# Attention scores and values by turns in the first unit of an attention and feed-forward kernel

## The chip, the cores and the metric

The kernel runs on one core of one Trainium2 chip. The metric is the device time of one execution in microseconds; the kernel before takes 1377.58 us (median of three runs, 1377.35 to 1379.76). A profiled execution spans 1376.2 us.

Names of engines: PE is the matrix engine (PEld its weight loads), ACT the scalar engine, DVE the vector engine, POOL GpSimd, SP the engine that issues DMA transfers. PE writes only to PSUM, which the kernel uses as eight banks of 128 partitions by 512 fp32 numbers, `banks[0]` to `banks[7]`.

## The reference

Attention with normalized q and k over 8 batches of 12 heads, 448 positions, 64 features, and behind it a feed-forward block with a squared ReLU. All is fp32.

```python
q_n, k_n = rmsnorm(q, g_q), rmsnorm(k, g_k)     # (8, 12, 448, 64)
scores = scale * np.matmul(q_n, k_n.transpose(0, 1, 3, 2))
attn = np.exp(scores - max); attn = attn / (sum(attn) + 1e-09)
x = np.matmul(attn, v)  # -> (8 * 448, 12 * 64) = (3584, 768)
h = np.maximum(x @ w_in, 0.0)                   # w_in (768, 2048)
out = h * h @ w_out                             # w_out (2048, 768)
```

## The kernel before, in words

**Pairs.** The unit of attention work is a pair of heads of one batch: 48 pairs, `i` = 0 to 47, six for each batch. The 128 partitions hold the two heads' 64 features (for q and k turned to features by positions), or 128 positions. A pair's 448 keys are three blocks of 128 (`m` = 0, 1, 2) and 64 last ones; the last keys of an even pair and of the odd pair behind it share one tile (`m` = NJ = 3). For a block, `score(i, m)` multiplies k and q into two banks (one for each head e), keys on the partitions; `weigh(i, m)` lets ACT read both banks and write the exps to two `wT` tiles (L466; a ring of eight). There is no maximum to subtract as long as the gains are small (`shift` is False; that is the path that runs). `attend(i, (n,))` multiplies the weights of a block with v and adds up in the values' bank (bank 4). `additions(i)` lets POOL add the weights of the blocks up (L485, two `sum` tiles), `denominators(i)` multiplies these sums with ones (L620), so that each sum stands in all 64 partitions of its head, and DVE transposes the bank by blocks (`take_sums`, L662). `invert(i)` takes reciprocals of one number for each position and spreads them again, and `finish(i)` multiplies the values with them.

**Order.** The order of all instructions is written out by hand. A feed-forward unit works on two batches; while its matmuls run, the attention of the next two batches is laid between them. `run(until)` takes steps of the feed-forward stream (a Python generator whose steps have costs) until a due place, and small tasks (queues `tasks`, `pool_tasks`) with each step. The stream of the first unit (L1021 matmuls for the first product, L1200 and L1286 for the second) also converts the weights: they arrive as 64-bit words by DMA (L1424, L1429) and three ACT steps (L1443, L1444, L1446) and two DVE steps (L1457, L1476) make fp32 of each piece.

Pairs 0 to 12 come ahead of the first unit. The attention of pairs 13 to 24 lies in the first unit (130 to 483 us of the span), in two half visits for each pair (`visit_among(i, n)`, n = 0 and 1), at equal distances of cost. Pairs 25 to 47 (`whole(i)` is `i > 24`) lie in the second unit in one visit each, `visit_whole(i)`.

**A first half visit** (n = 0) of pair i: values of blocks 0 and 1 of pair i-1, then scores and exps of blocks 0 and 1 of pair i. **A second half visit** (n = 1): values of block 2 of pair i-1, for odd i also the last keys of both pairs i-1 and i (`attend_both`, L586, which writes the odd pair's part to bank 2 and lets ACT copy it to a tile `rest`, L593), then score and exps of block 2 and, for even i, of the last keys, for which q and k of pair i+1 must be there. Some half a visit's distance ahead of the second half visit, between feed-forward products, stand `denominators(i - 1)`, in bank 3. Also just ahead of a second half visit stands the turning of the next pair's q (DVE, L370) and its scaling by ACT (L380).

**Shapes on PE.** In these visits a score of a block is two matmuls of 64 rows (features of a head) by 128 columns (keys), one for each head (L458); values are two of 128 rows (keys) by 64 columns (L550). Scores of block m go to banks 0 and 1 (m even) or 2 and 3 (m odd).

**The second unit before** already works in quarters: there a score is four matmuls of 64x64 (two heads, two halves of the keys, L447), values are four too (`attend_halves`, L565): the two halves of the keys add up in two banks, 4 and 3 (`second_bank`), which `join_halves` (L574 to 578) adds: for odd pairs DVE adds `rest` and then the second bank; for even pairs ACT copies `rest` from bank 0 and the values from bank 4 (L576, L577), then DVE adds the second bank (L578). `finish` then multiplies on POOL (L708), where the other form does it on DVE (L713, L715). In a visit, values of block m of pair i-1 and the score of block m of pair i take turns; the scores of blocks 0, 1, 2 and the last keys go to banks (0, 1), (2, 0), (1, 2) and (0, 4).

`joint(i)` (L280) says that a pair's values are in two banks; it is `whole(i - i % 2 + 1)`, so true from pair 24 on. `sums_bank(i)` (L525) is bank 3 in the first unit.

Of the kernel before, what the change touches and what calls it, by code (L numbers as in the profile page):

```python
# [26 lines left out]
NJ = 3  # L27
# [198 lines left out]
def program(ctx, tc, rows, v, g, wide, ones, moe_w_in, moe_w_out, out, shift):  # L226
# [50 lines left out]
    def whole(i):  # L277
        return i > 2 * 2 * NPAIR

    def joint(i):  # L280

        return whole(i - i % 2 + 1) and not shift

    def slots_of(i, n):

# [14 lines left out]
    def alone(i):  # L300

        return pairs[i][0] < 2
# [131 lines left out]

    def banks_of(i, m):

        if whole(i) and not shift:
            return [banks[n][:, 0:S] for n in ((0, 1), (2, 0), (1, 2), (0, 4))[m]]
        return [banks[m % 2 * 2 + e][:, 0:S] for e in range(2)]

    def score(i, m):

        scs = banks_of(i, m)
        if whole(i) and m < NJ:
            for e, sc in enumerate(scs):
                for half in range(2):
                    nc.tensor.matmul(  # L447
                        sc[ds(half * D, D)],
                        lhsT=turned[i, 1][ds(e * D, D), ds(m * P + half * D, D)],
                        rhs=turned[i, 0][ds(e * D, D), :], start=True, stop=True,  # L450
                    )
            return
        for p in (i, i + 1) if m == NJ else (i,):
            some = ds(p % 2 * LASTS, LASTS) if m == NJ else ds(0, P)
            keys = ds(m * P, LASTS if m == NJ else P)
            for e, sc in enumerate(scs):
                r = ds(e * D, D)
                nc.tensor.matmul(  # L458
                    sc[some], lhsT=turned[p, 1][r, keys], rhs=turned[p, 0][r, :],
                    start=True, stop=True,  # L460
                )
# [60 lines left out]
                nc.vector.tensor_copy(out=tiles[NJ][e][mine, part], in_=tr[mine, NJ, :size])  # L522

    def sums_bank(i):
        return banks[4 + (i + 1) % 2 if alone(i) else 2 if whole(i + 1) else 3][:, 0:S]  # L525

    def values_bank(i):
# [89 lines left out]
    def denominators(i):  # L617

        for e in range(2):
            nc.tensor.matmul(  # L620
                sums_bank(i)[ds(e * D, D), :], lhsT=ones, rhs=sums.pop((i, e)),
                start=True, stop=True,
            )
        take_sums(i)
# [1142 lines left out]

    def visit_among(i, n):
        run_all()
        if not shift:  # L1770
            if n and i - 1 not in inverse:
                denominators(i - 1)
            attend(i - 1, (2 * n, 2 * n + 1))
            forget(i - 1, (2 * n, 2 * n + 1))
        elif n == 0:
            attend_all(i - 1)
        if n == 0 and i <= last:
            load_v(i)
        if i <= last:
            weigh_slots(i, n)  # L1780
        if n and not shift:
            tasks.append(lambda: invert(i - 1))
            tasks.append(lambda: finish(i - 1))
        if n and i <= last and not shift:
            additions(i)
        if n == 0:
            prepare(i + 2)
            run_tasks(2)
            tasks.appendleft(lambda: None)
        elif whole(i + 1):  # L1790
            prepare(i + 3)

    def room_for_squares(i):

# [75 lines left out]
    with tc.manual_schedule(engines=ENGINES):  # L1870
# [8 lines left out]
        for i in range(len(pairs) + 1):  # L1879
            for n in range(1 if whole(i) else VISITS):  # L1880
                at = i * VISITS + n - VISITS - unit
                if at < 0:
                    visit_alone(i, n)
                    continue
                u, x = divmod(at, unit)
                if x == 0:
                    u, x = u - 1, unit
                run(place(u, x - (1 if whole(i - 1) else 0.5)))
                if i < last:
                    if whole(i) and not shift:  # L1890
                        tasks.append(partial(lambda i: turn_blocks(i + 1, 1), i))
                        tasks.append(partial(lambda i: turn_blocks(i + 1, 0), i))
                        tasks.append(partial(lambda i: load_qk(i + 4), i))
                    else:
                        for some in (1, 0) if whole(i) else (1 - n,):
                            turn_among(i + 1, some)
                        if n or whole(i):
                            tasks.append(lambda i=i: load_qk(i + 4))
                    if n and first and x > 1 and not shift:
                        denominators(i - 1)  # L1900
                run(place(u, x))
                if x == unit:
                    closing = whole(i)
                    drain()
                    stream, spent, first = ffn(u + 1), 0, u < 0
                    if shift:
                        run(COST if first else LATER)
                    elif first:
                        run(COST_IN + 1)
                slowly = x < unit  # L1910
                if whole(i):
                    visit_whole(i)
                else:
                    visit_among(i, n)
# [35 lines left out]
```

## Time and profile before

| what | value |
|---|---|
| median of three runs | 1377.58 us |
| span of the profiled execution | 1376.2 us |
| granted PE clock over the span | 0.999 |
| PE busy | 1351.8 us, 98% |
| ACT, DVE, POOL busy | 45%, 60%, 58% |
| first unit's stretch with attention (125 to 483 us): PE busy | 353.59 of 358 us |
| matmul lines of the visits there | L458 and L550, L586, L620 |
| the same in the second unit | L447, L565, L586, L458, L629 |

A busy PE here means that matmuls follow each other; shares are averages over stages, so the visits are looked at one by one: start of the first attention matmul to start of the first feed-forward matmul behind it. In a row of the timeline stand start, length, engine, line, operation, out<-in, shape, and in brackets idle time of the engine just before it and what ended that; several instructions of a kind are merged (x8). An fp32 matmul shows as two MATMUL instructions.

### The profile page before, as it was taken

What the parts mean: (1) busy time and instruction counts of PE and PEld (TensorE: products, weight loads), DVE (VectorE), ACT (ScalarE), POOL (GpSimd) and SP (SyncE); (2) the same over time, 40 slices, a digit from 0 to 9 for tenths busy, and PEclk for the clock granted to TensorE, in tenths of its full rate; (3) what the DMA queues carried; (4) which work ended last, traced back from release to release, by engine and by line L of the source; (5) the groups of instructions that cost most, each with busy time, mean ns of one, the idle gap of its engine ahead of it and who ended that gap; (6) DMA issues with size and microseconds to landing.
All of it is one profiled execution on the core that took longest, in us unless ns stands there. A gap on an engine that the chain in (4) does not pass through costs nothing.

```text
span 1376.2 us, 19610 instructions
## 1 busy us (share of the span) xinstructions
PE 1351.8 (98%) x6320; PEld 844.0 (61%) x6320; DVE 819.2 (60%) x1647; ACT 614.6 (45%) x1130; POOL 792.1 (58%) x792
## 2 busy tenths in 40 slices
PE   7999999999999999999999999999999999999998
PEld 3333444444444476677768586766767777868684
DVE  4897555877767765455547755455556642544454
ACT  6995476757757244442434244443524032203030
POOL 5668664755656878576767887565846630303030
PEclk9999999999999999999999999999999999999999
DMA  5665846977859866674748575665527441515133
GB/s 137 172 180 152 206 110 166 255 194 204 253 135 280 253 173 207 155 206 107 222 99 242 166 201 163 150 198 144 175 70 240 149 166 65 172 57 184 40 126 105
DMA packets 394372, 229.82 MB, mean 167 GB/s; under 512 B 271892, under 2 KB 355988, under 8 KB 393236
## 3 DMA queue, kind: packets, MB, share of 16 engines
q1 hardware_dynamic: 393968, 228.41, 58.8%
q8 instruction: 52, 0.85, 0.3%
q14 instruction: 60, 0.49, 0.1%
q10 hardware_dynamic: 292, 0.07, 0.0%
HBM read 171.05 MB, written 57.34 MB: 166 GB/s over the span
## 4 chain that ended last, share of the span: by engine, by line
PE 86%; DVE 3%; POOL 3%; issue 2%; ACT 2%; DMA 2%; SPq 1%; POOLq 0%; ACTq 0%; DVEq 0%
PE bank L1286 31%; PE bank L1077 25%; PE bank L1021 8%; PE bank L565 4%; PE bank L447 4%; PE bank L458 4%; PE bank L550 3%; PE bank L1200 2%; PE bank L586 1%; DMA in_sb<-in_deep 1%; PE bank L629 1%; PE bank L602 1%; PE bank L620 1%; DVE acc L1383 1%; SPq L159 1%
## 5 line engine op out<-in xcount | busy, mean ns | idle before, releaser
L1077 PE MATMUL bank<-xT,in_sb 128*128 128x224 f32 x1344 | 288.0, 353 | 0.0
L1286 PE MATMUL bank<-out_sb,hid 128*128 128x384 f32 x768 | 273.0, 488 | 2.0 <-POOL out_sb L1552 1.4
L1383 DVE TENSOR_TENSOR acc<-acc,bank 128x384 f32<-128x384 f32 x312 | 166.3, 548 | 160.0 <-PE bank L1286 131.4
L1077 PEld LDWEIGHTS bank<-xT,in_sb 128*128 128x128 f32 x1344 | 252.9, 190 | 10.4 <-ACT wT L466 5.6
L466 ACT ACTIVATE wT<-bank,rr 128x448 f32<-128x448 f32 x288 | 164.0, 632 | 157.9 <-PE bank L447 97.9
L1286 PEld LDWEIGHTS bank<-out_sb,hid 128*128 128x128 f32 x768 | 144.6, 190 | 104.4 <-issue 6.3
L1286 PE MATMUL bank<-out_sb,sums 128*128 128x384 f32 x576 | 207.0, 490 | 1.1 <-DVE acc L1383 0.7
L204 POOL TENSOR_TENSOR rr<-ms,minus_half 128x8 f32<-128x8 f32 (+1 forms) x96 | 145.3, 1514 | 69.1 <-DVE ms L197 65.8
L1062 DVE TENSOR_TENSOR hid<-hid,bank 128x224 f32<-128x224 f32 x312 | 111.3, 384 | 83.0 <-PE bank L1077 77.9
L1286 PEld LDWEIGHTS bank<-out_sb,sums 128*128 128x128 f32 x576 | 107.7, 190 | 86.0 <-DVE acc L1383 4.1
L1021 PE MATMUL bank<-xT,in_sb 128*128 128x448 f32 x336 | 131.7, 545 | 0.0
L485 POOL TENSOR_TENSOR sum<-sum,wT 128x448 f32<-128x448 f32 (+1 forms) x96 | 112.5, 1194 | 7.6 <-ACT wT L466 6.1
L458 PE MATMUL bank<-qT,kT 64*128 64x448 f32 (+1 forms) x492 | 102.4, 571 | 3.5 <-ACT qT L380 2.4
L1021 PEld LDWEIGHTS bank<-xT,in_sb 128*128 128x128 f32 x336 | 62.1, 190 | 68.8 <-issue 60.9
L1130 POOL TENSOR_TENSOR hid<-hid 128x448 f32<-128x448 f32 x24 | 27.3, 1144 | 123.1 <-DVE hid L1062 118.7
L485 POOL TENSOR_TENSOR sum<-wT 128x448 f32<-128x448 f32 x48 | 55.9, 1185 | 68.6 <-ACT wT L466 68.6
L1134 ACT ACTIVATE hid<-hid 128x448 f32<-128x448 f32 x96 | 55.0, 573 | 72.3 <-DVE hid L1062 48.4
L447 PE MATMUL bank<-qT,kT 64*64 64x448 f32 x552 | 75.1, 540 | 0.0
L1077 PE MATMUL bank<-more,in_sb 128*128 128x224 f32 x288 | 74.3, 353 | 0.0
L458 PEld LDWEIGHTS bank<-qT,kT 64*128 64x128 f32 (+1 forms) x492 | 35.3, 166 | 63.4 <-issue 37.1
L1074 ACT COPY hid<-bank 128x448 f32<-128x448 f32 x24 | 12.8, 533 | 136.9 <-PE bank L1077 136.1
L565 PE MATMUL bank<-wT,vt 64*64 64x448 f32 x576 | 73.3, 544 | 0.0
(142 smaller groups left out, 2063.1 us busy)
## 6 DMA issues: line engine op xcount, KB each, us to landing
out_sb<-out_forms SPq DMA_DIRECT2D x80, 384.0 KB, 5.2
in_sb<-in_deep SPq DMA_DIRECT2D x64, 384.0 KB, 4.1
in_sb<-in_deep SPq DMA_DIRECT2D x80, 256.0 KB, 4.2
words<-in_moe_w_in_dram SPq DMA_DIRECT2D x32, 384.0 KB, 3.9
words<-in_moe_w_out_dram SPq DMA_DIRECT2D x32, 384.0 KB, 3.6
out_forms<-out_sb SPq DMA_DIRECT2D x8, 1536.0 KB, 6.6
qk<-in_q_dram SPq DMA_DIRECT2D x96, 96.0 KB, 2.8
qk<-in_k_dram SPq DMA_DIRECT2D x96, 96.0 KB, 2.8
```

Of the source, the lines that this page charges most:

```text
L204: self.nc.gpsimd.tensor_tensor(out=self.rr[i][:, x, 0 : self.count(i)], in0=ms, in1=self.minus_half.to_broadcast(list(ms.shape)), op=ALU.pow,)
L447: nc.tensor.matmul(sc[ds(half * D, D)], lhsT=turned[i, 1][ds(e * D, D), ds(m * P + half * D, D)], rhs=turned[i, 0][ds(e * D, D), :], start ...
L458: nc.tensor.matmul(sc[some], lhsT=turned[p, 1][r, keys], rhs=turned[p, 0][r, :], start=True, stop=True,)
L466: nc.scalar.activation(new_weights((i, m), e), sc, AF.Exp, scale=rows.rr[i][:, 1, 2 * m + e : 2 * m + e + 1],)
L485: nc.gpsimd.tensor_tensor(out=sums[i, e][some], in0=left[some], in1=weights[key_of(i, m), e][some], op=ALU.add)
L565: nc.tensor.matmul(bank[ds(e * D, D), :], lhsT=values[i][keys, n, e, :], rhs=weights[(i, n), e][keys], start=n == 0, stop=n == NJ - 1 and ...
L1021: nc.tensor.matmul(ps, lhsT=w_sb[:, IN.index(left), c, :], rhs=forms[u, c][right], start=first and c == 0, stop=c == NK - 1, skip_group_ch ...
L1062: nc.vector.tensor_tensor(out=quarter(name, n), in0=quarter(base, n), in1=ps, op=ALU.add)
L1077: nc.tensor.matmul(ps, lhsT=left, rhs=right, start=start, stop=stop, skip_group_check=True)
L1134: nc.scalar.activation(dst, dst, AF.Relu)
L1286: nc.tensor.matmul(ps, lhsT=extra[left][:, t] if tt == NT else lefts[left][:, t, ts(tt, P)], rhs=w_sb[t][:, OUT.index(right), :], start=fi ...
L1383: nc.vector.tensor_tensor(out=acc, in0=acc, in1=ps, op=ALU.add)
```

## The change

Pairs 13 to 24 get the form of the second unit, in their two half visits:

- `quartered(i)`, `i > 12`, takes the place of `whole(i)` in `joint`, `banks_of` and `score`, so scores are quarters in banks (0, 1), (2, 0), (1, 2), (0, 4), and values from pair 12 on are halves in banks 4 and 3, with `join_halves` and POOL's multiplication in `finish`.
- A new `visit_quarters(i, n)` issues a half visit. n = 0: values 0, score 0, values 1, score 1, each score followed by its exps. n = 1: values 2, score 2, then for odd i both pairs' last values, then `join_halves(i - 1)`, for even i the score of the last keys, and at the end `denominators(i - 1)`.
- These denominators go to bank 1 in place of bank 3, and no longer stand ahead of the second half visit between feed-forward products.
- `load_v(i)` is called behind the first half visit's matmuls; nothing else is moved.

```diff
+    def quartered(i):
+        return i > 2 * NPAIR
+
     def joint(i):
-        return whole(i - i % 2 + 1) and not shift
+        return quartered(i - i % 2 + 1) and not shift
...
     def banks_of(i, m):
-        if whole(i) and not shift:
+        if quartered(i) and not shift:
             return [banks[n][:, 0:S] for n in ((0, 1), (2, 0), (1, 2), (0, 4))[m]]
...
     def score(i, m):
         scs = banks_of(i, m)
-        if whole(i) and m < NJ:
+        if quartered(i) and m < NJ:
...
     def sums_bank(i):
+        if joint(i) and not whole(i + 1):
+            return banks[1][:, 0:S]
         return banks[4 + (i + 1) % 2 if alone(i) else 2 if whole(i + 1) else 3][:, 0:S]
...
     def visit_among(i, n):
         run_all()
-        if not shift:
+        if quartered(i) and not shift:
+            visit_quarters(i, n)
+        elif not shift:
...
-        if i <= last:
+        if i <= last and (shift or not quartered(i)):
             weigh_slots(i, n)
...
+    def visit_quarters(i, n):
+
+        for m in range(NJ)[2 * n : 2 * n + 2]:
+            attend(i - 1, (m,))
+            forget(i - 1, (m,))
+            score(i, m)
+            weigh(i, m)
+        if n == 0:
+            return
+        if i % 2:
+            attend(i - 1, (NJ,))
+            forget(i - 1, (NJ,))
+        join_halves(i - 1)
+        if i % 2 == 0:
+            score(i, NJ)
+            weigh(i, NJ)
+        denominators(i - 1)
...
-                    if n and first and x > 1 and not shift:
-                        denominators(i - 1)
```

## The prediction

> **What bounds the kernel now.** The page comes first, for what the time hangs on.
>
> ```profile
> span 1376.2 us, 19610 instructions
> PE 1351.8 (98%) x6320; PEld 844.0 (61%) x6320; DVE 819.2 (60%) x1647; ACT 614.6 (45%) x1130; POOL 792.1 (58%) x792
> PE 86%; DVE 3%; POOL 3%; issue 2%; ACT 2%; DMA 2%; SPq 1%; POOLq 0%; ACTq 0%; DVEq 0%
> ```
>
> PE is busy for 98% of the span and carries 86% of the chain that ended last: a microsecond in which it stands still or works longer is a microsecond of the kernel. So I asked next, by windows, how long each attention visit of the first unit holds PE, from its first matmul to the first feed-forward matmul behind it. The first half visits of pairs 13 to 24 (pair 13's, those of pairs 17, 20 and 23, the sum of all twelve; a row is window, length, then busy PE, PEld, DVE, ACT, POOL):
>
> ```profile
> 131.54:134.90 3.36, 3.36 (x17) 1.17 (x16) 0.75 (x2) 0.54 (x1) 3.16 (x3) 1.00 0.59 94
> ...
> 246.74:250.10 3.36, 3.36 (x18) 1.18 (x17) 3.36 (x5) 1.31 (x3) 3.36 (x3) 1.00 0.96 231
> ...
> 335.14:338.50 3.36, 3.36 (x18) 1.17 (x17) 3.36 (x5) 0.03 (x1) 3.36 (x4) 1.00 1.05 271
> ...
> 424.98:428.34 3.36, 3.36 (x17) 1.17 (x16) 3.36 (x5) 2.69 (x5) 3.36 (x3) 1.00 1.13 305
> ...
> sum 40.32, PE 40.32 PEld 14.10 DVE 22.71 ACT 10.54 POOL 25.11; mean PE 3.36 PEld 1.17 DVE 1.89 ACT 0.88 POOL 2.09
> ```
>
> The sum is twelve times 3.36, with PE busy throughout and whatever the other engines do: here PE waits for nobody. Values of two key blocks come first, then two scores, which go to banks 0 to 3 that ACT emptied long ago. The second half visits, odd pairs, then even pairs:
>
> ```profile
> 141.86:145.94 4.08, 4.08 (x21) 1.30 (x20) 2.74 (x5) 1.20 (x2) 4.00 (x5) 1.00 0.96 284
> ...
> 260.41:263.18 2.77, 2.77 (x18) 0.71 (x17) 2.59 (x6) 2.27 (x5) 0.00 (x0) 1.00 1.15 433
> 320.90:323.67 2.77, 2.77 (x18) 0.71 (x17) 2.59 (x4) 1.22 (x3) 2.34 (x2) 1.00 1.05 297
> ...
> 438.66:441.43 2.77, 2.77 (x18) 0.71 (x17) 2.59 (x6) 1.87 (x4) 0.00 (x0) 1.00 1.05 346
> sum 17.93, PE 17.93 PEld 4.85 DVE 14.04 ACT 9.93 POOL 11.81; mean PE 2.99 PEld 0.81 DVE 2.34 ACT 1.66 POOL 1.97
> ```
>
> ```profile
> 171.18:175.79 4.61, 3.72 (x18) 0.89 (x17) 4.37 (x9) 3.71 (x7) 1.36 (x2) 1.00 0.11 25
> 231.78:235.26 3.48, 3.48 (x17) 0.89 (x16) 3.26 (x8) 2.06 (x4) 0.46 (x2) 1.00 1.03 286
> 291.53:294.30 2.77, 2.77 (x17) 0.71 (x17) 2.77 (x5) 1.48 (x3) 2.77 (x4) 1.00 0.78 191
> ...
> 470.01:472.78 2.77, 2.77 (x18) 0.71 (x17) 1.89 (x5) 1.49 (x3) 2.69 (x3) 1.00 0.46 94
> sum 22.33, PE 19.95 PEld 4.98 DVE 20.74 ACT 15.89 POOL 9.88; mean PE 3.33 PEld 0.83 DVE 3.46 ACT 2.65 POOL 1.65
> ```
>
> The odd ones are 2.77 us (pair 13's 4.08 holds its denominators too). The even ones run from 2.77 (pairs 18 and 24) to over 4.61; what lengthens them is priced below.
>
> **The new form where nothing is late.** The second unit of the same run already works by turns on quarters, so its timeline prices the new form: one visit, with the exps of its first score.
>
> ```profile
> 483.29 0.98 PE L565 MATMUL bank<-wT,vt 64*64 64x448 f32 x8
> 484.09 0.93 PE L447 MATMUL bank<-qT,kT 64*64 64x448 f32 x8
> 484.85 0.93 PE L565 MATMUL bank<-wT,vt 64*64 64x448 f32 x8
> 485.14 1.16 ACT L466 ACTIVATE wT<-bank,rr 128x448 f32<-128x448 f32 x2 [4.04 <-PE bank L447]
> 485.83 0.97 PE L447 MATMUL bank<-qT,kT 64*64 64x448 f32 x6
> ```
>
> A group (the values or the score of one key block) takes 0.80 us at the start of a visit and 0.76 each behind another. The second score writes banks 2 and 0, and bank 0 still holds the first score's first head. The exp that empties it starts 1.85 us into the visit (485.14), and the second score's second head starts 0.69 after that, at 2.54 (485.83), though its turn was at 0.80+2x0.76 = 2.32. So even here, where ACT had nothing else to do (4.04 us of idle time ahead of the exp), PE is held a little by ACT. Three more rows give what follows a late start, and what denominators cost by themselves:
>
> ```profile
> 174.89 0.97 PE L458 MATMUL bank<-qT,kT 64*64 64x448 f32 x4 [0.89 <-ACT qT L380]
> ...
> 463.41 0.97 PE L620 MATMUL bank<-sum,ones 128*64 128x448 f32 x4
> 464.31 1.88 PE L1286 MATMUL bank<-out_sb,sums 128*128 128x384 f32 x5
> ```
>
> Quarters that start afresh at 174.89 hold PE until 175.79, the end of that window: 0.90. Denominators, both heads in two passes, hold it 0.90 too (463.41 to 464.31).
>
> **First half visits.** Four groups by turns replace four groups in a row: the same number of passes through the array, with twice the instructions for a score. With ACT free the visit is 2.54+0.90 = 3.44 long in place of 3.36: +0.08. So the turns gain nothing here, and they put an exp into PE's path. PE takes its instructions in order (in pair 14's window, 171.18, it runs 3.72 of 4.61 us and none of the feed-forward matmuls fills the rest): when the second score's second head waits, so do all matmuls behind it, and through them DVE and ACT. What counts now is when the first exp can run:
>
> ```profile
> ACT wT L466 <- PE bank L458: 28.9, 11, 13.7
> 135.52 0.64 ACT L466 ACTIVATE wT<-bank,rr 128x448 f32<-128x448 f32 x1 [3.34 <-POOL sum L485]
> 248.76 0.56 ACT L1443 ACTIVATE words<-words 128x384 f32<-128x384 f32 x1 [2.89 <-DMA words<-in_moe_w_out_dram]
> 250.64 1.67 ACT L466 ACTIVATE wT<-bank,rr 128x448 f32<-128x448 f32 x3
> ...
> 338.47 0.56 ACT L1443 ACTIVATE words<-words 128x384 f32<-128x384 f32 x1 [4.19 <-DMA words<-in_moe_w_out_dram]
> 340.33 2.20 ACT L466 ACTIVATE wT<-bank,rr 128x448 f32<-128x448 f32 x4
> ...
> 426.60 1.07 ACT L1446 ACTIVATE words<-words 128x384 f16<-128x384 f32 x1
> ```
>
> In the first unit ACT's exps mostly waited for their scores (11 waits), ACT having nothing else to do; so I count eight visits at 0.08, 0.64. Four are late. Pair 13: POOL still reads the weights that the exp overwrites, exp at 135.52, 3.98 into the visit; with 0.69 until bank 0 is written and 0.90 from there it makes 5.57, +2.21. Pairs 17 and 20: three ACT steps on a weight load that is still landing stand ahead of the exp, which starts at 3.90 and 5.19: 5.49 and 6.78, +2.13 and +3.42. Pair 23: those steps end at 427.67, 2.69 in: 4.28, +0.92. In the trace of before these late exps cost nothing: no matmul of the visit needs them. First half: 0.64+2.21+2.13+3.42+0.92 = +9.3 us.
>
> **Second half visits, odd pairs.** Three groups (values, score, both pairs' last values), and then the denominators that stood by themselves ahead of the visit. They go to bank 1, which holds the third score's first head, so they too wait for an exp. Promptly: exp at 1.85, denominators from 2.54 to 3.44; before, 2.77+0.90 = 3.67. But ACT scales the next pair's q ahead of that exp:
>
> ```profile
> 263.41 0.65 ACT L380 ACTIVATE qT<-qT,g 128x448 f32<-128x448 f32 x1
> 322.84 0.67 ACT L380 ACTIVATE qT<-qT,g 128x448 f32<-128x448 f32 x1 [1.55 <-DVE qT L370]
> 441.66 0.65 ACT L380 ACTIVATE qT<-qT,g 128x448 f32<-128x448 f32 x1
> ```
>
> It ends 3.65 into the visits of pairs 17 and 23 and 2.61 into pair 19's. With 0.69+0.90 behind it: 5.24, 5.24 and 4.20. The other three I take as prompt, 3x3.44 = 10.32; were they as late as pair 19's, it would be 2.3 more. After 25.0, before 17.93+5x0.90 = 22.43: +2.6 us.
>
> **Second half visits, even pairs.** The last score needs the next pair's scaled q:
>
> ```profile
> 233.64 0.67 ACT L380 ACTIVATE qT<-qT,g 128x448 f32<-128x448 f32 x1 [1.42 <-DVE qT L370]
> ```
>
> In pair 16's visit q is ready at 234.31, and the visit ends 0.95 later, at 235.26; in pair 14's PE waits 0.89 for it outright (174.89). q's time is set by DVE and ACT, which the change leaves as they are up to there, so four visits end when they did, and the denominators behind them find bank 1 read. Only pairs 18 and 24 (2.77) can be shorter: three groups are 0.80+0.76+0.90 = 2.46, but the last score's second head goes to the values' bank, and DVE must have read that. Between 0 and 0.3 each; I take 0.1: -0.2 us.
>
> **Work that moves.** POOL gets a multiplication for each pair in place of DVE's. The denominators, now behind the visit instead of ahead of it, keep the two sum buffers longer, which POOL's next additions need. POOL's queue stops at both.
>
> ```profile
> L708 POOL TENSOR_TENSOR xT<-xT,inverse x12: 1127/1137/1525, 519.2 to 1076.5; 128x448 f32<-128x448 f32 x12
> POOL sums L1186 <- ACT hid L1170: 42.7, 8, 8.4
> ```
>
> That is 12x1.14 = 13.7 us more on an engine that stood 42.7 us waiting for ACT in this stretch. I take 0, that wait being the cover; without it see the last rival. For even pairs ACT copies one more bank (not longer than a late exp's 0.64) beside feed-forward matmuls: 0. DVE stands at the transposition of the sums until the denominators are done, and the feed-forward additions stand behind it; the feed-forward part has three banks in turn, so I take 0. The loads of v are issued behind the visit's instructions now, but nothing else is issued on SP's queue in between: 0. Bounds of all this together: -2 (PE's delays let loads land in time for the next exp) and +5.
>
> **Sum.** 9.3+2.6-0.2 = +11.7 us on the span of 1376.2, so 1387.9; the median, 1377.58, lies 1.4 above that span, so 1389.3.
>
> **Rivals.** *Faster: the change of shape is what costs.* The groups at 484.09 and 484.85 are 0.76 apart without a change of shape; four such are 3.04, so the three changes of shape in a 3.36 visit cost 0.32, or 0.1 each. If ACT were never waited for, first halves would be 2.32+0.90 = 3.22 (12x0.14 = 1.7 saved), odd second halves 2.46+0.90 = 3.36 (22.43-6x3.36 = 2.3), even ones 0.6 less: 4.6 saved, 1373.0. It decides if the exp is over by 2.3 us into a visit; 485.83 says that it isn't even in the quiet second unit. 6%. [...]
>
> *No difference: the four late exps go away*, as PE's own delays give POOL and the loads time. Then 12x0.08 = +1.0, odd pairs 6x3.44-22.43 = -1.8, even -0.2: -1.0, 1376.6. Against it: ACT's three steps follow feed-forward work that shifts with PE. 10%.
>
> *Slower still: POOL's queue.* In pairs 14, 17, 20 and 23 second products follow the visit and read sums from POOL:
>
> ```profile
> 183.63 2.74 PE L1286 MATMUL bank<-out_sb,sums 128*128 128x384 f32 x8
> ```
>
> That is 12.4 us after 171.18. If the four sums stand behind the multiplication and two additions, POOL starts it at some 5.2+3 us (an estimate: pair 17's denominators, then three DVE steps of about an exp's length, and their waits), and ends seven steps of 1.14 later, at 16.2: 3.8 us late in four places, 15 us, 1404. It decides if the sums are issued behind the multiplication; by the code they are issued with the next product, ahead of it. 8%.
>
> **Numbers.** Forecast 76%. Its own range is 1384 to 1395 (two of the late exps away; +5 behind the visits). For 8 in 10 I take 1381 to 1397. A measurement of this kernel tells about 0.2%, 2.7 us. Faster 6%, same 10%, slower 84%.
>
> **What would show it.** Right: first half visits of 3.4 us with outliers of 4 to 7 us at pairs 13, 17, 20 and 23, where PE's idle time ends by the exp (ACT wT); odd second halves with denominators over 5 us at pairs 17 and 23; the second unit as before. Wrong: PE without waits for ACT wT in the first unit, or visits no longer than now; or new waits at feed-forward matmuls for POOL sums or DVE.

## The result and the profile after

The changed kernel takes 1395.68 us (median of four runs, 1394.06 to 1396.95), the kernel before 1377.46 us beside it (1377.2 to 1379.76): the ratio is 1.0126, 95% interval 1.0112 to 1.0141. That is 18.2 us slower, where 11.7 were forecast. The range, 1381 to 1397, holds it; the narrower one that I gave to the sum itself, 1384 to 1395, ends 0.7 below it. The profiled execution spans 1395.0 us, 18.8 more than before.

Lines of the kernel after stand 3 to 5 lower than before: the exps are L469 (L466), scores L450 in quarters and L461 in whole (L447, L458), denominators L625 (L620), `join_halves` L579 to L583 (L574 to L578), ACT's scaling of q L383 (L380), the conversion L1448 to L1451 on ACT and L1481 on DVE, ACT's steps on hidden values L1174 and L1175, feed-forward matmuls L1026 and L1291.

Page of the kernel after, its span, busy times and chain by engine:

```profile
span 1395.0 us, 20218 instructions
PE 1356.8 (97%) x6608; PEld 849.4 (61%) x6608; DVE 833.9 (60%) x1647; ACT 618.5 (44%) x1136; POOL 807.2 (58%) x804
PE 75%; DVE 6%; POOL 4%; issue 4%; DMA 4%; SPq 3%; ACT 3%; POOLq 0%; ACTq 0%; DVEq 0%
```

PE is busy 5.0 us longer than before, so most of the 18.8 us is PE standing still. Its share of the chain has fallen from 86% to 75%: other engines now stand in it.

Kernel after, windows on the twelve first half visits (window, length, then busy PE, PEld, DVE, ACT, POOL, granted clock, DMA; pairs 13, 14, 17, 20, 23 and the sum):

```profile
131.89:137.46 5.57, 4.12 (x33) 1.29 (x32) 1.09 (x3) 1.66 (x3) 5.37 (x5) 1.00 0.64 110
161.82:165.26 3.44, 3.44 (x34) 1.29 (x33) 2.51 (x3) 1.30 (x3) 3.44 (x3) 1.00 0.84 187
...
250.49:255.81 5.32, 4.12 (x33) 1.29 (x32) 5.32 (x6) 3.40 (x6) 5.32 (x5) 1.00 0.78 195
...
344.08:350.21 6.13, 4.48 (x33) 1.29 (x32) 6.13 (x7) 3.49 (x6) 6.13 (x6) 0.94 0.83 208
...
438.22:442.55 4.33, 4.13 (x33) 1.29 (x33) 4.33 (x5) 3.43 (x6) 4.33 (x4) 1.00 1.12 330
...
sum 48.76, PE 44.26 PEld 15.52 DVE 32.13 ACT 23.11 POOL 34.80; mean PE 3.69 PEld 1.29 DVE 2.68 ACT 1.93 POOL 2.90
```

Eight visits are at 3.41 to 3.44 us, four are late, and PE runs only 4.1 to 4.5 us of the 4.3 to 6.1 that these last. (Part of the waiting is inside these busy times: pair 23's visit has as many matmuls as a prompt one and counts 4.13 in place of 3.41 to 3.44 us, because one head's matmuls run on while the other's wait.) The same for the second half visits, which now hold the denominators: odd pairs (17, 23, sum of six), then even pairs (18, 24, sum of six).

```profile
265.03:270.25 5.22, 3.39 (x29) 1.05 (x28) 2.64 (x5) 5.16 (x10) 1.98 (x3) 1.00 1.08 379
...
451.77:457.37 5.60, 3.39 (x29) 1.04 (x29) 3.20 (x7) 4.32 (x9) 2.99 (x3) 1.00 1.04 375
sum 26.19, PE 20.33 PEld 6.28 DVE 12.80 ACT 20.82 POOL 9.14; mean PE 3.39 PEld 1.05 DVE 2.13 ACT 3.47 POOL 1.52
```

```profile
297.90:303.11 5.21, 4.28 (x30) 1.18 (x29) 3.96 (x8) 2.42 (x5) 2.39 (x2) 1.00 0.78 167
...
484.84:489.86 5.02, 4.28 (x30) 1.18 (x29) 3.74 (x7) 2.54 (x5) 4.94 (x6) 1.00 0.56 118
sum 30.00, PE 27.11 PEld 7.80 DVE 19.86 ACT 22.25 POOL 12.10; mean PE 4.52 PEld 1.30 DVE 3.31 ACT 3.71 POOL 2.02
```

Kernel after, what PE waited for in the first unit's stretch (125 to 505 us of the span; us in total, times, longest):

```profile
PE bank L625 <- ACT wT L469: 5.6, 4, 2.2
PE bank L450 <- ACT wT L469: 4.5, 4, 1.6
PE bank L461 <- DVE xT L579: 2.6, 3, 0.9
PE bank L1291 <- POOL out_sb L1557: 2.0, 3, 0.7
PE bank L1291 <- DVE acc L1388: 1.3, 3, 0.6
...
```

Kernel before, the same question (125 to 483 us of its span):

```profile
PE bank L458 <- ACT qT L380: 2.4, 2, 1.5
PE bank L1286 <- POOL out_sb L1552: 1.4, 2, 0.7
PE bank L1286 <- DVE acc L1383: 0.6, 2, 0.3
```

All three kinds of wait at the top of the first list are new: 5.6 us of denominators (L625) and 4.5 us of second scores (L450) waiting for an exp, 2.6 us of last scores (L461) waiting for DVE's first step of `join_halves` (L579).

Where the time went, after less before, from the sums above (before: 40.32, 17.93 and 22.33, with five sets of denominators at 0.90 for the odd and six for the even pairs):

| part of the span | us |
|---|---|
| ahead of pair 13 | +0.35 |
| first half visits, 48.76 - 40.32 | +8.4 |
| odd second half visits, 26.19 - 22.43 | +3.8 |
| even second half visits, 30.00 - 27.73 | +2.3 |
| stretches between the visits | +2.25 |
| second unit (one wait of 1.56 us for a load of weights) | +1.9 |

They add up to 19.0, by which the last visit starts later; the end of the span is 18.8 later. The stretches between visits hold things that go opposite ways. Eleven of them no longer have denominators standing alone and are 0.20 us shorter each. And in two of them PE ran at half its clock for a while. Windows of the stretch between pair 13's two visits, kernel after, then kernel before:

```profile
137.46:146.12 8.66, 8.66 (x21) 4.01 (x19) 4.68 (x9) 3.71 (x8) 6.55 (x6) 0.80 0.68 189
```

```profile
135.40:142.36 6.96, 6.96 (x20) 3.21 (x18) 5.65 (x10) 4.73 (x9) 6.96 (x7) 1.00 0.55 129
```

The same matmuls, PE busy throughout, take 8.66 in place of 6.96 us (+1.70), at a granted clock of 0.80 in place of 1.00. The record of the clock shows half speed from 137.80 to 141.21, 3.41 us, and again from 349.43, behind pair 20's late exp. Most of what is left of the stretches is PE waiting at second products of the feed-forward block (L1291) for POOL and DVE: 3.3 us in the first list above, 2.0 in the second.

### The profile page after: what moved, and what is told of

It reads as the page before. It is cut to its first block, busy times and chain, and to the rows that moved or that the text cites. A ratio compares the mean times of both kernels' runs of the same rounds, so it can differ in the third digit from the quotient of the medians.

```text
span 1395.0 us, 20218 instructions
## 1 busy us (share of the span) xinstructions
PE 1356.8 (97%) x6608; PEld 849.4 (61%) x6608; DVE 833.9 (60%) x1647; ACT 618.5 (44%) x1136; POOL 807.2 (58%) x804
## 4 chain that ended last, share of the span: by engine, by line
PE 75%; DVE 6%; POOL 4%; issue 4%; DMA 4%; SPq 3%; ACT 3%; POOLq 0%; ACTq 0%; DVEq 0%
PE bank L1291 29%; PE bank L1082 25%; PE bank L450 5%; PE bank L570 5%; PE bank L1026 5%; PE bank L1205 2%; PE bank L461 1%; DMA words<-in_moe_w_in_dram 1%; SPq L332 1%; POOL sum L488 1%; POOL rr L204 1%; PE bank L634 1%; DVE acc L1388 1%; PE bank L591 1%; DVE more L1517 1%
## 5 line engine op out<-in xcount | busy, mean ns | idle before, releaser
L1291 PE MATMUL bank<-out_sb,hid 128*128 128x384 f32 x768 | 273.5, 488 | 4.8 <-POOL out_sb L1557 2.0
L1388 DVE TENSOR_TENSOR acc<-acc,bank 128x384 f32<-128x384 f32 x312 | 166.7, 549 | 149.5 <-PE bank L1291 134.6
L469 ACT ACTIVATE wT<-bank,rr 128x448 f32<-128x448 f32 x288 | 165.3, 631 | 163.9 <-PE bank L450 144.2
L1291 PEld LDWEIGHTS bank<-out_sb,hid 128*128 128x128 f32 x768 | 144.4, 190 | 108.4 <-issue 9.7
L1291 PE MATMUL bank<-out_sb,sums 128*128 128x384 f32 x576 | 206.6, 489 | 1.1 <-DVE acc L1388 0.6
L1291 PEld LDWEIGHTS bank<-out_sb,sums 128*128 128x128 f32 x576 | 108.0, 190 | 84.3 <-issue 4.2
L1026 PE MATMUL bank<-xT,in_sb 128*128 128x448 f32 x336 | 132.7, 553 | 0.0
L450 PE MATMUL bank<-qT,kT 64*64 64x448 f32 x840 | 114.8, 541 | 4.5 <-ACT wT L469 4.5
L570 PE MATMUL bank<-wT,vt 64*64 64x448 f32 x864 | 108.1, 547 | 0.0
L1026 PEld LDWEIGHTS bank<-xT,in_sb 128*128 128x128 f32 x336 | 64.0, 194 | 68.9 <-issue 67.2
L461 PE MATMUL bank<-qT,kT 64*64 64x448 f32 (+1 forms) x348 | 73.2, 571 | 4.2 <-DVE xT L579 2.6
L450 PEld LDWEIGHTS bank<-qT,kT 64*64 64x64 f32 x840 | 42.9, 132 | 52.2 <-issue 40.9
```

What stands on the lines that cost most here:

```text
L450: nc.tensor.matmul(sc[ds(half * D, D)], lhsT=turned[i, 1][ds(e * D, D), ds(m * P + half * D, D)], rhs=turned[i, 0][ds(e * D, D), :], start ...
L461: nc.tensor.matmul(sc[some], lhsT=turned[p, 1][r, keys], rhs=turned[p, 0][r, :], start=True, stop=True,)
L469: nc.scalar.activation(new_weights((i, m), e), sc, AF.Exp, scale=rows.rr[i][:, 1, 2 * m + e : 2 * m + e + 1],)
L570: nc.tensor.matmul(bank[ds(e * D, D), :], lhsT=values[i][keys, n, e, :], rhs=weights[(i, n), e][keys], start=n == 0, stop=n == NJ - 1 and ...
L1026: nc.tensor.matmul(ps, lhsT=w_sb[:, IN.index(left), c, :], rhs=forms[u, c][right], start=first and c == 0, stop=c == NK - 1, skip_group_ch ...
L1291: nc.tensor.matmul(ps, lhsT=extra[left][:, t] if tt == NT else lefts[left][:, t, ts(tt, P)], rhs=w_sb[t][:, OUT.index(right), :], start=fi ...
```

## The experiments

My theory after this comparison: before, PE ran ahead of ACT and DVE in these visits; the change ties it to their queues by reusing banks at once (bank 0 in first halves, bank 1 for denominators, bank 4 for the last score), and what it meets there is mostly the conversion of the weights, which waits for transfers. The main rival: the quarters and turns cost by themselves. A second question was whether the costs add up visit by visit or come back elsewhere when one is removed. All times stand against the kernel before on the same chip; "shift" is by how much pair 25's visit starts later than before in the profiled execution (after: 17.1 us).

| kernel | median us | ratio, 95% interval | half clock, us |
|---|---|---|---|
| after | 1395.68 | 1.0126, 1.0112 to 1.0141 | 6.8 |
| denominators between products | 1397.54 | 1.0139, 1.0122 to 1.0156 | 13.7 |
| quarters without turns | 1400.25 | 1.0159, 1.0142 to 1.0176 | 3.4 |
| conversion held | 1397.12 | 1.0133, 1.0116 to 1.0150 | 20.5 |
| score first | 1394.57 | 1.0116, 1.0099 to 1.0133 | 10.2 |
| from pair 15 | 1393.72 | 1.0104, 1.0088 to 1.0119 | 17.1 |
| q behind the visit | 1395.35 | 1.0118, 1.0102 to 1.0133 | 10.2 |
| after, no weight loads | 1391.21 | 1.0092, 1.0076 to 1.0107 | 10.2 |
| before, no weight loads | 1379.41 | 1.0010, 1.0001 to 1.0019 | 0 |
| after, no conversion | 1389.36 | 1.0086, 1.0072 to 1.0101 | 13.7 |
| before, no conversion | 1378.54 | 1.0005, 0.9996 to 1.0014 | 0 |
| before, denominators at every visit | 1377.52 | 0.9998, 0.9989 to 1.0007 | 6.8 |
| before, denominators at odd visits | 1375.66 | 0.9987, 0.9978 to 0.9996 | 0 |

The last column is how long the record of the clock shows half speed in the first unit, in the one execution that was profiled (the kernel before: 0). By the two windows above, half of such a spell is lost where PE is busy in it: an estimate of 3.4 us for the changed kernel, and of some 8 us for "conversion held" and "from pair 15". So part of the time that comes back in the experiments below comes back through the clock, and not through longer waits. Where work is left out of the changed kernel, and with denominators at every visit, the profiled execution was 3.8 to 6.0 us above the median, so there the column does not hold for the median.

### Denominators back between the products

```diff
     def visit_quarters(i, n):
+        if n and i - 1 not in inverse:
+            denominators(i - 1)
...
-        denominators(i - 1)
...
+                    if n and first and x > 1 and not shift:
+                        denominators(i - 1)
```

> The changed kernel with the denominators put back between feed-forward products, half a place ahead of the second half visit (bank 1 kept). Theory (PE waits behind exps whose bank it needs again): the odd second halves no longer wait for the third score's exp; with their denominators they held PE 26.2 us after the change and should hold it about 21 (6 x (2.5 + 0.9)), the isolated denominators give back about 0.2 us each of change of shape: 3 to 4 us faster than the changed kernel, about 1392. Rival (the quarter form itself, its extra instructions and joins, costs the time): no difference, 1395.7.

It took 1397.54 us, 5 more than expected. The odd second halves did what was expected (1.7 us less than before in all, where the changed kernel has 3.8 more), but the shift is 19.5: the time came back, most of it between the visits. Its waits in the first unit:

```profile
PE bank L450 <- ACT wT L469: 4.7, 3, 2.6
PE bank L1291 <- DVE acc L1388: 3.7, 5, 1.4
...
PE bank L1291 <- POOL out_sb L1557: 1.8, 1, 1.8
```

No denominators wait any more; second products of the feed-forward block (L1291) wait instead, and the clock went to half four times for 3.41 us each in this unit. So removing the denominators' waits, 5.6 us in the changed kernel, bought nothing; of the 5 us against the expectation some 3 are half clock (an estimate: half of 13.7 less half of 6.8).

### Quarters without turns

```diff
-        for m in range(NJ)[2 * n : 2 * n + 2]:
-            attend(i - 1, (m,))
-            forget(i - 1, (m,))
+        some = range(NJ)[2 * n : 2 * n + 2]
+        attend(i - 1, some)
+        forget(i - 1, some)
+        for m in some:
             score(i, m)
             weigh(i, m)
```

> The changed kernel with the same quarters and banks, but first half visits in the old order: both values, then both scores. Theory: the first score's exp now has no group of values to run beside, so in the eight prompt visits PE stands about 0.75 us more for bank 0 (3.4 becomes 4.2 us), the four late ones stay: 6 us slower than the changed kernel, about 1402. Rival (quarters themselves): same instructions, no difference, 1395.7.

1400.25 us, near what the theory expects. Windows of the first half visits (pair 14, and the sum):

```profile
160.40:164.59 4.19, 4.12 (x34) 1.29 (x33) 2.58 (x3) 1.59 (x3) 4.11 (x4) 1.00 0.84 209
...
sum 54.58, PE 49.48 PEld 15.53 DVE 32.27 ACT 25.28 POOL 35.91; mean PE 4.12 PEld 1.29 DVE 2.69 ACT 2.11 POOL 2.99
```

With nothing between a score and the score that reuses its bank, a prompt visit is 4.19 us where by turns it is 3.44 and before 3.36. The second score's second head starts 0.69 us behind the start of the exp (163.69 and 163.00), as the prediction has it; the profile counts PE as busy meanwhile, since the first head's matmuls run on. The quarters are the same; what differs is how much of the exp PE sees. So the exposed exp is the cost, and the turns hide part of it.

### Scores first

```diff
+        if n == 0:
+            score(i, 0)
+        attend(i - 1, some)
+        forget(i - 1, some)
         for m in some:
-            attend(i - 1, (m,))
-            forget(i - 1, (m,))
-            score(i, m)
+            if m:
+                score(i, m)
             weigh(i, m)
```

> The changed kernel with first half visits in the order score 0, values 0, values 1, score 1: the first score's exp gets two groups of values to run beside in place of one. Theory: the prompt visits lose their last wait (3.4 becomes 3.2 us, 8 x 0.2), the four late ones end as late as before, since their exp is held by something outside the visit: 1.5 to 2 us faster than the changed kernel, about 1394. Rival (quarters themselves): no difference, 1395.7.

1394.57 us, as expected, though its interval overlaps the changed kernel's. First half visits, windows of pairs 14 and 17:

```profile
161.61:164.78 3.17, 3.17 (x33) 1.13 (x33) 2.68 (x3) 1.16 (x2) 3.15 (x3) 1.00 0.87 194
...
249.83:254.90 5.07, 4.12 (x33) 1.29 (x32) 5.07 (x5) 3.42 (x6) 5.07 (x5) 1.00 0.75 188
```

With two groups of values to hide the exp, even pairs' prompt visits last 3.17 us, less than before the change. Odd pairs' prompt ones stay at 3.43 to 3.49. The late ones stay late (pair 17's is 5.07, 5.32 in the changed kernel): an exp that ACT had not begun was not hidden by 0.8 us of other matmuls.

### The conversion held back

```diff
-            while first and late and late[0] <= spent:
+            while first and late and late[0] <= spent < quiet:
...
+                quiet = float("inf") if n else place(u, x) - 12
                 run(place(u, x - (1 if whole(i - 1) else 0.5)))
```

> The changed kernel with the conversion of a weight piece held back when it is due within 12 units of cost ahead of a first half visit (pairs 17, 20 and 23), until behind the visit. Theory: the exps of these visits are prompt, the visits shrink from 5.3, 6.1 and 4.3 us to 3.4, and the half clock after pair 20's goes (1.7 us): 6 to 7 us faster than the changed kernel, about 1389. Rival (quarters themselves, or work behind the visits): no difference, 1395.7.

1397.12 us: no gain. The first half visits of pairs 17, 20 and 23 became prompt as meant (3.41 to 3.44), but the held pieces then met the second half visits. ACT and PE at pair 17's, from the timeline of this kernel:

```profile
266.27 0.54 ACT L1448 ACTIVATE words<-words 128x384 f32<-128x384 f32 x1 [3.18 <-DMA words<-in_moe_w_in_dram]
...
270.84 1.14 ACT L469 ACTIVATE wT<-bank,rr 128x448 f32<-128x448 f32 x2
```

```profile
271.60 1.76 PE L625 MATMUL bank<-sum,ones 128*64 128x448 f32 x4 [6.47 <-ACT wT L469]
```

In these rows ACT takes its instructions in order: it stands 3.18 us for a transfer while the bank is ready, and PE's denominators wait 6.47 us (10.8 us of such waits in the unit, 5.6 in the changed kernel).

### No weight loads, and no conversion

Two pairs of kernels leave work out. In the first, the loads of weight words are left out after the first three pieces, and later pieces are converted again from those three; in the second, ACT's three conversion steps are left out too for the later pieces.

```diff
     def load_weights(n):
...
+        if n > 2:
+            words[n] = words_kept[n % 3]
+            return
         kind, t, form, rows = all_pieces[n]
-        words[n] = new_words()
+        words[n] = words_kept[n] = new_words()
...
     def split_words(n):
-        if n not in words:
+        if n not in words or n > 2:
             return
```

(The last edit is in the second pair alone.)

> The changed kernel, with the loads of weight words left out after the first three pieces: all later pieces are converted again from the same three buffers, so the weights are not the reference's and ACT's, DVE's and POOL's steps on them stay, but none of them waits for a transfer. Theory (PE now waits for exps that stand in ACT's queue behind a conversion whose words are still landing): the first half visits of pairs 17, 20 and 23 come down from 5.3, 6.1 and 4.3 us to 3.4 to 4, pair 13's stays at 5.6 with its half clock behind it, odd second halves lose 2 to 3 us, and the kernel stands 3 to 8 us above the kernel before with the same part left out: about 1382. Rival (the turns cost by themselves, through ACT's and DVE's own work, whatever the loads do): the difference between the two kernels without loads stays 14 us or more: 1391 or above.

> The kernel before with the same part left out (no loads of weight words after the first three pieces). In the kernel before PE waited in this stretch 1.4 us for sums that POOL makes of the weights and 2.4 us for q: by both theories it gets faster by no more than about 1.5 us, 1376.8, since nothing that PE multiplies there waits for the words directly.

> The changed kernel with no loads of weight words after the first three pieces, and with ACT's three conversion steps left out for all later pieces too (47 pieces x 2.18 us = 102 us of ACT's time in this stretch): DVE's and POOL's steps go on, on the same three converted pieces, so the weights are not the reference's. If the conversion, loads and steps together, is what holds the exps: against the kernel before with the same part left out the difference falls from the 11.8 us that were left without the loads to 3 to 7 us (about 1384), all first halves but pair 13's at 3.4 to 3.5 us, and what is left stands at pair 13, at pairs 18 and 24 (DVE) and at pairs 17 and 23, where ACT's four steps on the hidden values stand ahead of the exp. If the coupling costs the same whatever stands in ACT's queue: 10 us or more.

> The kernel before with the same parts left out. Without the loads alone it took 1379.4 us; PE did not wait for the conversion there, so by both theories this one takes the same, 1376 to 1380 us.

The kernel before hardly moves (1379.41 and 1378.54 us; the first 1.3 above the kernel before beside it, where 1.5 or less below was expected; its trace shows one new wait of 1.2 us for a load in the second unit). The changed kernel without loads is 11.8 us above it (1391.21), without the conversion 10.8 (1389.36), where 18.2 was the difference with everything. Without the loads, the difference lies between the two answers; without the conversion, the second answer holds, 10 us or more whatever stands in ACT's queue, and my theory that PE meets mostly the conversion there is refuted, as far as the loads and ACT's steps go (DVE's and POOL's steps of the conversion stayed). The transfers are at most about a third of the loss (6.4 us, with some 3 us of uncertainty by the intervals), and part of this third is the clock: the four executions of the changed kernel had a granted clock of 0.996 or 0.997, three of the four without loads 0.999, as the kernel before. The conversion's 102 us of ACT time beside them is worth nothing that these runs can tell, and more than half of the loss is something else. What that is, the trace of the changed kernel without conversion shows (its profiled execution was 4.1 us above its median, so it tells places better than sizes). Its waits in the first unit:

```profile
PE bank L625 <- ACT wT L469: 7.1, 4, 3.0
PE bank L461 <- DVE xT L579: 3.8, 3, 2.1
PE bank L450 <- ACT wT L469: 1.5, 1, 1.5
```

The first halves are prompt but for pair 13's; the denominators wait longer than with the conversion. ACT and PE at pair 23's second half:

```profile
449.96 0.58 ACT L1174 ACTIVATE hid<-hid 128x448 f32<-128x448 f32 x1 [2.00 <-DVE hid L1168]
450.57 0.58 ACT L1175 ACTIVATE hid<-hid 128x448 f32<-128x448 f32 x1
451.06 0.56 ACT L1174 ACTIVATE hid<-hid 128x448 f32<-128x448 f32 x1
451.65 0.58 ACT L1175 ACTIVATE hid<-hid 128x448 f32<-128x448 f32 x1
452.13 0.65 ACT L383 ACTIVATE qT<-qT,g 128x448 f32<-128x448 f32 x1
452.69 1.14 ACT L469 ACTIVATE wT<-bank,rr 128x448 f32<-128x448 f32 x2
```

```profile
453.45 0.97 PE L625 MATMUL bank<-sum,ones 128*64 128x448 f32 x4 [3.04 <-ACT wT L469]
```

This visit stands right behind the end of a first product. ACT has been idle for 2.00 us, waiting for DVE to add that product up; then its four steps on the hidden values and the scaling of q, about 2.7 us, stand ahead of the exp. The score was ready all the while. This wait is mostly the feed-forward block's own chain, not ACT's conversion.

### The new form from pair 15 on

```diff
     def quartered(i):
-        return i > 2 * NPAIR
+        return i > 2 * NPAIR + 2
```

> The changed kernel with pairs 13 and 14 left as before (the new form from pair 15 on). If costs add up visit by visit: pair 13's first half gives back 2.2 us, the half clock behind it 1.7, its second half 0.2, against 0.4 for two sets of denominators that stand by themselves again: 3.7 us less than the changed kernel, about 1392. If a wait that is taken away in one place comes back in the next (PE being ahead of the weights' conversion by as much): 1394.5 to 1396.

1393.72 us (1390.49 to 1395.07), between the two answers, and its interval reaches both. In the profiled execution pair 13 and 14 give back all they cost: pair 15's second half visit starts 2.3 us earlier than before the change, where the changed kernel's starts 3.2 later. But at pair 25 the shift is 16.5 in place of 17.1. ACT ahead of pair 20's exps, the changed kernel, then this one:

```profile
346.42 0.57 ACT L1448 ACTIVATE words<-words 128x384 f32<-128x384 f32 x1 [3.22 <-DMA words<-in_moe_w_out_dram]
```

```profile
343.31 0.55 ACT L1448 ACTIVATE words<-words 128x384 f32<-128x384 f32 x1 [4.00 <-DMA words<-in_moe_w_out_dram]
```

PE came to this visit 3.9 us earlier (at 340.17, not 344.08), the transfer landed only 3.1 earlier, and PE waited 2.42 us for the exp in place of 1.65, with 6.83 us of half clock behind it in place of 3.41. In that execution, the longest of the four, the gain came back as longer waits and as half clock, 17.1 us in place of 6.8; by the medians about 2 us of it stayed, which the intervals can't tell from nothing or from all.

### q turned behind the visit

```diff
-                        for some in (1, 0) if whole(i) else (1 - n,):
+                        behind = n and i % 2 and quartered(i) and not (whole(i) or shift)
+                        for some in (1, 0) if whole(i) else () if behind else (1 - n,):
...
                     visit_among(i, n)
+                    if n and i % 2 and quartered(i) and i < last and not shift:
+                        turn_among(i + 1, 0)
```

> The changed kernel with one thing moved: in the second half visits of odd pairs the turning of the next pair's q, and its scaling by ACT (0.65 us), stand behind the visit in place of ahead of it. If ACT's queue ahead of the exp sets the denominators, those visits get 0.6 us shorter at pairs 17, 19 and 23, 1.8 us in all: about 1394. If the time goes back into the next waits: 1395.5.

1395.35 us: no difference from the changed kernel that can be told. Its waits in the first unit:

```profile
PE bank L450 <- ACT wT L469: 5.9, 4, 3.4
PE bank L625 <- ACT wT L469: 3.1, 2, 1.7
```

The visits of pairs 17, 19 and 23 did get shorter, by 0.39, 0.55 and 0.54 us, and pair 13's by 0.7: the 5.6 us of denominators are 3.1. So what stands ahead of the exp on ACT does set them. But pair 20's first half now waits 3.41 us where it waited 1.65, and its visit takes 8.3 us.

### One part of the change, on the kernel before

The denominators, in their old form and bank, directly ahead of the second half visit in place of half a place earlier: for all pairs, and for odd pairs alone.

```diff
-                    if n and first and x > 1 and not shift:
-                        denominators(i - 1)
```

```diff
-                    if n and first and x > 1 and not shift:
+                    if n and first and x > 1 and not shift and i % 2 == 0:
```

> The kernel before with one thing of the change alone: the denominators no longer stand by themselves between feed-forward products, but directly ahead of the second half visit, same bank and same form. In the changed kernel each such place was 0.2 us shorter without them. Theory: the change of shape costs that much, so 11 places give 2.2 us, 1376. Rival: the reciprocals come later by half a place, values stay in their bank longer, and nothing or less than nothing is left: 1378 or above.

> The kernel before, with the denominators put directly ahead of the second half visit of odd pairs alone (six places; even pairs keep them between feed-forward products). With all pairs changed, the odd visits with their denominators had got 0.15 us shorter and the stretch ahead of each 0.2, but the visits of pairs 18, 20 and 24 longer. If those even pairs took the gain: 6 x 0.35 = 2.1 us less than before, 1376. If there is none: 1378.

For all pairs: 1377.52 us, no difference. The stretches are 0.2 us shorter, as in the changed kernel, but even pairs' last score goes to the denominators' bank, and pair 20's waits:

```profile
PE bank L458 <- DVE inverse L662: 1.2, 1, 1.2
```

For odd pairs alone, where no score follows in that bank: 1375.66 us, ratio 0.9987, as expected. Its odd second half visits but pair 13's, which held its denominators already (pair 15's is shown), hold 3.52 us with the denominators, where 2.77 and 0.90 were 3.67:

```profile
201.41:204.93 3.52, 3.52 (x22) 0.99 (x21) 1.81 (x3) 2.19 (x4) 3.48 (x4) 1.00 1.08 219
```

PE is busy throughout; nobody is waited for. This is the only version faster than the kernel before, by about 2 us.

## Why the prediction was right, and where its sum was off

**Right: the mechanism of the first half visits.** Forecast +9.3, measured +8.4. Pair 13's visit came out at 5.57 (forecast 5.57), pair 17's at 5.32 (5.49), pair 20's at 6.13 (6.78), pair 23's at 4.33 (4.28), the other eight at 3.41 to 3.44 (3.44). PE waits there for the exp by the waits view, and the kernel without turns shows that the exposed exp is the price. Pairs 17 and 20 are a little under the forecast (pair 20's 6.13 even holds some 0.36 us of half clock: its last quarters take 1.26 us, 348.95 to 350.21, and 0.90 elsewhere), and both start later than before; that the loads gained on ACT there was not tested.

**Right in kind, 1.2 short: odd second halves.** Forecast +2.6, measured +3.8. Pairs 17 and 19 fit (5.22 for 5.24, 4.09 for 4.20). Pair 23 took 5.60 for 5.24, and pair 13's, which I counted as prompt at 3.44, took 4.23; with q turned behind the visit it takes 3.51, so there too q's scaling stood ahead of the exp. The bound that I gave for the prompt ones, 2.3, covers this.

**The step that failed: even second halves.** Forecast -0.2, measured +2.3. I wrote of pairs 18 and 24 that DVE must have read the values' bank, "between 0 and 0.3 each". They cost 1.54 and 1.35 us more than before, denominators counted on both sides. Of the four that I took as unchanged, three are, and pair 20's is 0.61 shorter (5.51 for 5.22 and 0.90): PE waits there 0.92 us for the same step of DVE, where it waited 1.49 for q. PE and DVE at pair 18's, kernel after:

```profile
301.30 0.98 PE L461 MATMUL bank<-qT,kT 64*64 64x448 f32 x6 [0.93 <-DVE xT L579]
```

```profile
298.95 0.63 DVE L373 STREAM_TRANSPOSE qT<-qk 128x448 f32<-128x448 f32 x1
299.51 0.51 DVE L1388 TENSOR_TENSOR acc<-acc,bank 128x384 f32<-128x384 f32 x1
299.95 0.76 DVE L1481 CUSTOM_DVE_ANT_0 in_sb<-words,in_sb 128x768 uint16<-128x768 uint16 x1
300.63 0.61 DVE L579 TENSOR_TENSOR xT<-bank,rest 128x448 f32<-128x448 f32 x1
```

Between q's transposition, whose times I had followed, and the read of the bank stand one DVE step of the feed-forward block (L1388) and one of the conversion (L1481). I had named the read, but priced neither it nor DVE's queue ahead of it, although I had done just that for ACT.

**Missing terms.** Of the 7.1 us that the sum was short on the span, 2.8 are in the visits; the rest is in terms that it did not have. It had no term for the clock: two spells of half clock, 1.7 us for the first by the two windows above, 3.4 for both (an estimate). It had no term for the 0.2 us that eleven stretches gain without isolated denominators; I had a price for a change of shape, 0.1, and put it only into a rival. And it had none for waits in the second unit (+1.9, one load of weights).

**Moved work, taken as 0.** POOL's extra multiplications: PE's waits for POOL's sums went from 1.4 to 2.0 us, and those for DVE's additions at the same matmuls from 0.6 to 1.3. That is the sign of being wrong that I named last, new waits at feed-forward matmuls for POOL or DVE, at a size of 1.3 us, within the 5 that I allowed. The rival with POOL's queue (1404 us) did not come about.

**The rivals.** The gain that I put down to fewer changes of shape exists (0.2 us in each of eleven places, and 3.17 us for a visit with scores first; no run varied the shape alone), but it is 2.2 us in all, against 12.7 us of waits of the three new kinds in the first list above. As to "the late exps go away": the four visits are late after the change, as forecast. Without loads the first halves of pairs 17, 20 and 23 are prompt, and the kernel is still 11.8 us slower; in its profiled execution denominators and last scores wait more (7.5 and 3.9 us, for 5.6 and 2.6).

**What stays open.** The 10.8 us that are left without conversion are waits for ACT's and DVE's feed-forward steps and pair 13's wait for POOL, by the trace; how they divide was not isolated, and no run took the hidden values' steps away from ahead of the exp. The clock has little part in them: three of the five executions had a granted clock of 0.999, as the kernel before, and took 1388.25 to 1389.36 us. No run kept the quarters and turns and gave the second score and the denominators banks that nobody else had just filled, which would try the reuse of banks by itself. Why an earlier PE finds the next wait longer was read from single executions.

## What to carry to other kernels

When a matmul takes over a bank that was just filled by another, price the queue of the engine that empties it, step by step, up to the read: an instruction that nobody waited for can be microseconds late for free (before the change pair 20's first exp began 5.19 us into its visit) until the change makes somebody wait. Do this for every engine that the new order ties PE to, DVE as much as ACT. And where PE runs ahead of other engines, do not add up gains visit by visit: in four variants here the time that a removed wait should have given back went to other waits or to spells of half clock, so judge by the whole stretch.

## What the runs showed of the hardware that was not expected

The granted clock of PE fell to half in the middle of a busy stretch, in spells of 3.41 us or twice that (6.83, in the kernels from pair 15 and with denominators at every visit). In the changed kernel's profiled execution this followed waits of 1.45 and 1.65 us, the ones ahead of 137.46 and 350.21, and not those of 1.83 and 2.21; between the two spells the clock is full for 208.21 us. Windows of the kernel after just behind the 1.65 and the 2.21 us wait:

```profile
350.21:353.60 3.39, 3.39 (x8) 1.79 (x7) 3.39 (x5) 2.19 (x4) 2.44 (x2) 0.61 0.70 233
457.40:460.80 3.40, 3.40 (x13) 2.07 (x12) 3.03 (x6) 0.30 (x1) 1.96 (x2) 1.00 0.62 155
```

Clock 0.61 behind the shorter wait, 1.00 behind the longer. A wait of 1.17 us in the kernel before with denominators at every visit was followed by 6.83 us of half clock, one of 3.12 us in the changed kernel without loads by none; the kernels that keep PE busy (before, and with denominators at odd visits) show it nowhere in the first unit of their profiled executions. In the kernel without turns the wait at the same place as the changed kernel's first, 1.44 us long, was followed by none. So in these executions a wait cost its own length and sometimes 1.7 us more (8.66 in place of 6.96 us above), or, by an estimate for the spells of 6.83 us, twice that. This shows in whole executions: of the eleven with denominators at odd visits, nine had a granted clock of 0.999 or above and took 1374.82 to 1376.25 us; those at 0.998 and 0.997 took 1377.87 and 1379.46. What decides whether a wait is followed by a spell, these runs don't show.
